# GateLoop attention and a multiplicative feed-forward block on one core: channels ordered (d h), gate tiles by parity of the unit, table functions in a fixed order

## The chip, the cores and the metric

The kernel runs on one NeuronCore of a Trainium2 chip. The metric is the device time of one execution in microseconds (us). PE is the matrix engine, DVE the vector engine, ACT the engine for table functions, POOL GpSimd, SP the engine whose queue issues most transfers.

## What is computed

Batch 4, 8 heads, 768 steps, 48 channels per head; then 3072 tokens of width 384 go through a feed-forward block of width 1024. The weights arrive in double precision, all else in float32.

```python
mag = np.sqrt(a_re * a_re + a_im * a_im)
scale = np.minimum(mag, 0.999) / (mag + 1e-06)
a_re_n, a_im_n = (a_re * scale, a_im * scale)
for t in range(S):
    new_re = ar * S_re - ai * S_im
    new_im = ar * S_im + ai * S_re
    S_re, S_im = (new_re + kv, new_im)
    y[:, :, t] = np.einsum('bhd,bhde->bhe', q[:, :, t], S_re)
...
a = x @ w1
b = x @ w2
h = a * b @ w3
return (h @ w_out).astype(np.float32)
```

## The kernel before

The work is cut into 8 units: a batch, half of its 768 steps (384), all heads. For each unit there are three kinds of work.

**Gates** (`gates`, L442 to L557). The 384 channels of all heads lie as 3 x 128 rows, 384 steps in the free direction. A chain of table functions (ACT), products and scans (DVE, POOL) turns the gates into decay and angle of every step and rotates q and k with them. The results are four tiles: k by cosine (`gR`), k by sine (`k`), q by cosine (`gA`), q by sine (`q`). `gZ` is scratch. All of `gA`, `gR`, `gZ`, `q`, `k` have one buffer, `re` and `im` two. The last lines of `gates` move the four tiles into a layout by head, `KL` and `QL`, with 2 x 48 rows and the head in the free direction. Channels are ordered (h d), so a head's 48 rows cross the borders of 128-row blocks and 40 transfers per unit are issued on SP (L551). Behind them on SP stand the loads of k and q of the next unit, and of the gates of the one after.

**Attention** (`scores`, `outputs`). For each of 3 chunks of 128 steps: transposes of `gR` and `k` (tp, L569) that ACT copies out (KT, L570), score products (sc, L574) that DVE masks (L575), outputs (y, L592 to L603) that ACT copies to xT (L605), and the state (kv on PE, T on DVE) for the next chunk.

**Feed-forward** (`ffn_ab`, `ffn_out`). Eight times a pair of products with w1 and w2 (m, L627), of which ACT copies one out (`a`) and DVE multiplies (`ab`, L632); then three output blocks (o, L637), copied by ACT and stored from ACT's own queue (L642).

Ahead of the units, the weights are converted from double to float32 in 36 pieces of at most 128 x 512 values (`convert`, L650 to L667: two operations on ACT, two on DVE, one on POOL, one on DVE), w3 and w_out are multiplied into one matrix (f, L719), and the gates of unit 0 run between them.

The program is written as: attention of unit u woven with the feed-forward of unit u-1 and the gates of unit u+1. The order on each engine is then chosen by the scheduler of the tile framework from its own estimates; engines and queues execute strictly in that order. The table functions on ACT belong to sets; a function of another set than the loaded one has an ACT_TABLE_LOAD in front of it.

```python
        nc.scalar.preload_act_table_set("natural_log_exp_and_others")
        for s in parts:
            act(out=A[:, s], in_=re[:, s], func=AF.Ln)
            act(out=r[:, s], in_=A[:, s], func=AF.Exp, scale=-1.0)
...
        nc.scalar.preload_act_table_set("trig_and_small")
        for s in parts:
            act(out=im[:, s], in_=im[:, s], func=AF.Arctan)
```

Of the kernel before, what the change touches and what calls it, by code (L numbers as in the profile page):

```python
# [15 lines left out]
PSUM = bass.MemoryType.PSUM  # L16

# [297 lines left out]
def kernel(  # L315
# [44 lines left out]
    KD = DM // P  # L360
    KF = FF // P
# [4 lines left out]
    LN_MAX = math.log(0.999)  # L366
# [20 lines left out]


# [23 lines left out]
    def rows(src, b):  # L412
        return src[b].rearrange("h d s -> (h d) s").rearrange("(f p) s -> p f s", p=P)

    def load_gates(u):
        b, h = divmod(u, 2)
        g = g_t[u] = {}
        for n, src in (("re", art), ("im", ait)):
            g[n] = two.tile([P, KD, TT], FP, tag=n, name=n)
            nc.sync.dma_start(out=g[n], in_=rows(src, b)[:, :, h * TT:(h + 1) * TT])  # L420

    def load_qkv(u):
        b, h = divmod(u, 2)
        g = g_t[u]
        g["q"] = one.tile([P, KD, TT], FP, tag="q", name="q")
        g["k"] = one.tile([P, KD, TT + UC], FP, tag="k", name="k")
        nc.sync.dma_start(out=g["k"][:, :, 0:TT], in_=rows(kt, b)[:, :, h * TT:(h + 1) * TT])
        nc.sync.dma_start(out=g["q"], in_=rows(qt, b)[:, :, h * TT:(h + 1) * TT])
# [12 lines left out]

    def gates(u, split):  # L442
# [3 lines left out]
        A, R = one.tile([P, KD, TT], FP, tag="gA", name="gA"), one.tile([P, KD, TT + UC], FP, tag="gR", name="gR")  # L446
# [5 lines left out]
        act = nc.scalar.activation  # L452
# [5 lines left out]
        nc.scalar.preload_act_table_set("natural_log_exp_and_others")  # L458
# [52 lines left out]
        nc.scalar.preload_act_table_set("trig_and_small")  # L511
# [28 lines left out]
        KL = two.tile([2 * D, H, TT + UC], FP, tag="KL", name="KL")  # L540
        QL = two.tile([2 * D, H, TT], FP, tag="QL", name="QL")
        L_t[u] = QL, KL, R, K2
        for dst, src in ((KL, (R, K2)), (QL, (A, q))):
            for hd in range(H):
                for x in range(2):
                    r0 = hd * D
                    while r0 < (hd + 1) * D:
                        f, p0 = divmod(r0, P)
                        n = min((hd + 1) * D - r0, P - p0)
                        d0 = x * D + r0 - hd * D  # L550
                        nc.sync.dma_start(out=dst[d0:d0 + n, hd], in_=src[x][p0:p0 + n, f])  # L551
                        r0 += n
        if u + 1 < NU:
            load_qkv(u + 1)
# [4 lines left out]
    def scores(u, c):  # L559
# [5 lines left out]
        for x, src in enumerate((R, K2)):  # L565
            if not last:
# [3 lines left out]
                nc.scalar.copy(out=KT[:, :, x], in_=tp.rearrange("p f c -> p (f c)").rearrange("p (h d) -> p h d", d=D))  # L570
# [63 lines left out]
    def ffn_out(u, t):  # L634
# [7 lines left out]
        nc.scalar.dma_start(out=out[r0:r0 + P, :], in_=o)  # L642
# [4 lines left out]
    LOAD = 512  # L647
    MIN_SQ = (1.125 * 2.0 ** -15) ** 2

    def convert(dst, pieces):  # L650

        r, m = dst.shape[1:]
        raw = two.tile([P, r, m, 2], I32, tag="raw", name="raw")
# [172 lines left out]
```

## Time and profile before

| | us |
|---|---|
| three runs | 766.9, 767.99, 768.14 (median 767.99) |
| the profiled execution's own time | 768.78 |
| its span in the trace | 767.0 |
| PE busy / DVE / ACT / POOL | 597.2 / 384.7 / 348.0 / 152.2 |

The profile tells for each engine when it was busy, what ended the idle time before an instruction, and which chain of work ended last. A busy PE is modelled time: matmuls overlap. A float32 matmul leaves two records on PE, a transpose one. "SPq" is the issue of transfers on SP.

### The profile page before, as it was taken

What the parts mean: (1) busy time and instruction counts of PE and PEld (TensorE: products, weight loads), DVE (VectorE), ACT (ScalarE), POOL (GpSimd) and SP (SyncE); (2) the same over time, 40 slices, a digit from 0 to 9 for tenths busy, and PEclk for the clock granted to TensorE, in tenths of its full rate; (3) what the DMA queues carried; (4) which work ended last, traced back from release to release, by engine and by line L of the source; (5) the groups of instructions that cost most, each with busy time, mean ns of one, the idle gap of its engine ahead of it and who ended that gap; (6) DMA issues with size and microseconds to landing.
All of it is one profiled execution on the core that took longest, in us unless ns stands there. A gap on an engine that the chain in (4) does not pass through costs nothing.

```text
span 767.0 us, 9438 instructions
## 1 busy us (share of the span) xinstructions
PE 597.2 (78%) x3514; PEld 376.7 (49%) x3514; DVE 384.7 (50%) x555; ACT 348.0 (45%) x466; POOL 152.2 (20%) x149
## 2 busy tenths in 40 slices
PE   0027795439599779879995899499888998899997
PEld 0013473215256446645663576257545655476554
DVE  4898737673424672485248336724671378131110
ACT  9977866543315542745263447334533463100110
POOL 5564313712202200230033011301120111000000
PEclk9999997658799999998999899789999999999999
DMA  8434545102335123312322240234013201300001
GB/s 298 143 110 156 182 123 171 56 27 90 111 95 187 52 58 88 116 49 75 110 81 77 70 148 11 73 101 126 11 34 93 82 11 33 94 20 11 23 0 35
DMA packets 49079, 65.81 MB, mean 86 GB/s; under 512 B 7552, under 2 KB 46464, under 8 KB 49024
## 3 DMA queue, kind: packets, MB, share of 16 engines
q1 hardware_dynamic: 45568, 60.40, 26.1%
q10 hardware_dynamic: 3456, 4.72, 1.7%
q8 instruction: 30, 0.49, 0.3%
q14 instruction: 25, 0.20, 0.1%
HBM read 41.42 MB, written 4.72 MB: 60 GB/s over the span
## 4 chain that ended last, share of the span: by engine, by line
PE 23%; DVE 21%; ACT 17%; SPq 15%; issue 13%; POOL 6%; DMA 4%; ACTq 0%; DVEq 0%; POOLq 0%
SPq L551 14%; PE m L627 12%; PE o L637 5%; DVE gZ L517 4%; DVE gZ L501 3%; DVE gR L487 3%; POOL cf L666 3%; POOL im L464 2%; PE sc L574 2%; PE kv L610 2%; ACT gZ L473 1%; DVE cf L665 1%; ACT L478 1%; ACT gZ L478 1%; DVE w3s L667 1%
## 5 line engine op out<-in xcount | busy, mean ns | idle before, releaser
L627 PE MATMUL m<-xT,w1s 128*128 128x384 f32 x384 | 153.2, 528 | 31.9 <-DVE w1s L667 14.6
L627 PE MATMUL m<-xT,w2s 128*128 128x384 f32 x384 | 148.0, 517 | 9.8 <-DVE w2s L667 4.9
L637 PE MATMUL o<-w3o,ab 128*128 128x384 f32 x384 | 130.1, 489 | 0.0
L627 PEld LDWEIGHTS m<-xT,w1s 128*128 128x128 f32 x384 | 74.0, 205 | 80.8 <-DVE w1s L667 17.4
L632 DVE TENSOR_TENSOR ab<-m,a 128x384 f32<-128x384 f32 x64 | 35.3, 554 | 140.8 <-PE m L627 140.6
L719 PE MATMUL f<-wo_s,w3s 128*128 128x384 f32 x128 | 50.0, 541 | 70.1 <-DVE w3s L667 70.1
L627 PEld LDWEIGHTS m<-xT,w2s 128*128 128x128 f32 x384 | 74.1, 200 | 59.5 <-issue 7.0
L631 ACT COPY a<-m 128x384 f32<-128x384 f32 x64 | 30.3, 477 | 149.2 <-PE m L627 134.7
L637 PEld LDWEIGHTS o<-w3o,ab 128*128 128x128 f32 x384 | 70.8, 190 | 45.1 <-issue 1.6
L719 PEld LDWEIGHTS f<-wo_s,w3s 128*128 128x128 f32 x128 | 25.4, 208 | 92.6 <-DVE w3s L667 75.3
L666 POOL TENSOR_TENSOR cf<-cf,low 128x512 int32<-128x512 int32 (+1 forms) x36 | 48.7, 1351 | 91.9 <-DVE cf L665 55.7
L574 PEld LDWEIGHTS sc<-QL,KL 96*128 96x128 f32 x384 | 51.8, 192 | 23.7 <-issue 12.2
L574 PE MATMUL sc<-QL,KL 96*128 96x128 f32 x384 | 56.7, 281 | 5.3 <-DMA QL<-q 4.5
L575 DVE COPY_PREDICATED A<-causal,sc 128x512 f32<-128x512 int32 x48 | 34.0, 732 | 47.2 <-PE sc L574 46.9
L439 POOL COPY V<-vr 128x128 f32<-128x128 f32 x24 | 10.6, 442 | 202.2 <-PE y L592 121.2
L528 ACT ACTIVATE re<-gZ 128x1152 f32<-128x1152 f32 (+1 forms) x10 | 9.6, 969 | 71.3 <-DVE gZ L525 71.3
L569 PE MATMUL tp<-ident,gR 128*128 128x128 f32 x60 | 12.2, 311 | 33.0 <-DVE gR L533 32.5
L464 POOL TENSOR_TENSOR im<-im,gR 128x1152 f32<-128x1152 f32 (+1 forms) x10 | 20.5, 2059 | 77.5 <-ACT gR L461 77.1
L610 PEld LDWEIGHTS kv<-V,KT 128*96 128x96 f32 x320 | 32.4, 174 | 5.1 <-issue 4.3
L610 PE MATMUL kv<-V,KT 128*96 128x64 f32 x320 | 34.1, 257 | 0.2 <-DVE T L614 0.2
L504 POOL TENSOR_TENSOR q<-q,gA 128x1152 f32<-128x1152 f32 (+1 forms) x10 | 21.8, 2182 | 60.4 <-DVE gA L498 60.4
L640 ACT COPY ot<-o 128x384 f32<-128x384 f32 x24 | 11.3, 474 | 48.8 <-PE o L637 48.1
(101 smaller groups left out, 837.8 us busy)
## 6 DMA issues: line engine op xcount, KB each, us to landing
raw<-in_w_dram SPq DMA_DIRECT2D x16, 512.0 KB, 3.8
re<-in_a_re_dram SPq DMA_DIRECT2D x8, 576.0 KB, 6.6
im<-in_a_im_dram SPq DMA_DIRECT2D x8, 576.0 KB, 3.8
k<-in_k_dram SPq DMA_DIRECT2D x8, 576.0 KB, 4.1
q<-in_q_dram SPq DMA_DIRECT2D x8, 576.0 KB, 5.6
vr<-in_v_dram SPq DMA_DIRECT2D x8, 576.0 KB, 4.2
out_dram<-ot ACTq DMA_DIRECT2D x24, 192.0 KB, 1.9
raw<-in_w_dram SPq DMA_DIRECT2D x32, 128.0 KB, 2.7
```

The lines of the kernel that those rows point to most:

```text
L464: nc.gpsimd.tensor_tensor(out=im[:, s], in0=im[:, s], in1=r[:, s], op=OP.mult)
L517: nc.vector.tensor_tensor_scan(out=Z[:, f], data0=im[:, f], data1=im[:, f], initial=0.0 if h == 0 else st_ang[:, u - 1, f, UC - 1:UC], op0 ...
L551: nc.sync.dma_start(out=dst[d0:d0 + n, hd], in_=src[x][p0:p0 + n, f])
L574: nc.tensor.matmul(out=sc[:, j], lhsT=KL[:, hd, w], rhs=QL[:, hd, w], start=True, stop=True)
L575: nc.vector.copy_predicated(out=A[:, x * H // 2:(x + 1) * H // 2], data=sc, mask=causal.rearrange("p (h t) -> p h t", h=1).to_broadcast([P ...
L610: nc.tensor.matmul(out=kv[:, hd], lhsT=KT[:, hd], rhs=V[:, hd], start=True, stop=True)
L627: nc.tensor.matmul(out=m, lhsT=w[:, f, j * P:(j + 1) * P], rhs=xT_t[u][:, f], start=(f == 0), stop=(f == KD - 1))
L631: nc.scalar.copy(out=a, in_=got[0])
L632: nc.vector.tensor_tensor(out=ab_t[u][:, j], in0=got[1], in1=a, op=OP.mult)
L637: nc.tensor.matmul(out=m, lhsT=ab_t[u][:, f, t * P:(t + 1) * P], rhs=w3o[:, f], start=(f == 0), stop=(f == KF - 1))
L666: nc.gpsimd.tensor_tensor(out=b, in0=b, in1=low, op=OP.add)
L719: nc.tensor.matmul(out=m, lhsT=w3_t[j][:, f], rhs=wo_s[:, f], start=(f == 0), stop=(f == KF - 1))
```

## The change

- The 384 channels of q, k and the gates are loaded in the order (d h): block f holds channels 16f to 16f+15 of all 8 heads (`load_rows`; three transfers per tile). A move to the head layout is then one transfer of 128 rows into 16 rows x 8 heads: 12 per unit.
- `gA`, `gR`, `q`, `k`, `KL`, `QL` of even units come from one pool, those of odd units from another (`sides`). The odd pool is opened when the conversions are over and lies where their scratch lay. `gZ` keeps one buffer. k and q of unit u+2 are requested when the gates of unit u+1 begin.
- The table functions of `gates` are chained: the scheduler must keep them in written order.
- The decay is accumulated as a product: exp ahead of the scan, minimum with 0.999, then a scan that multiplies; the correction step behind the scan (an Exp, a Ln, two DVE operations per unit) goes.
- Weights are converted in 18 pieces, mostly 128 x 1024, three raw buffers, one transfer each; the gates of unit 0 take a step at every piece.
- Outputs are stored from SP's queue.

```diff
+    def load_rows(dst, src, u):
+        b, h = divmod(u, 2)
+        for f in range(KD):
+            nc.sync.dma_start(out=dst[:, f, 0:TT], in_=src[b, :, DG * f:DG * (f + 1), h * TT:(h + 1) * TT].rearrange(
+                "h d s -> d h s"))
...
-        g["q"] = one.tile([P, KD, TT], FP, tag="q", name="q")
-        g["k"] = one.tile([P, KD, TT + UC], FP, tag="k", name="k")
+        g["q"] = sides[u % 2].tile([P, KD, TT], FP, tag="q", name="q")
+        g["k"] = sides[u % 2].tile([P, KD, TT + UC], FP, tag="k", name="k")
...
+    def chain(ins):
+
+        if chained:
+            tc.add_manual_dep(ins.ins, chained[-1].ins.name, ORDER, reason="tables")
+        chained[:] = [ins]
...
-        A, R = one.tile([P, KD, TT], FP, tag="gA", name="gA"), one.tile([P, KD, TT + UC], FP, tag="gR", name="gR")
+        A = sides[u % 2].tile([P, KD, TT], FP, tag="gA", name="gA")
+        R = sides[u % 2].tile([P, KD, TT + UC], FP, tag="gR", name="gR")
...
+        if 0 < u < NU - 1:
+            load_qkv(u + 1)
+        chain(nc.scalar.preload_act_table_set("natural_log_exp_and_others"))
...
-            ts(out=A[:, s], in0=A[:, s], scalar1=LN_MAX, scalar2=None, op0=OP.min)
-        for s in parts:
+            act(out=A[:, s], in_=A[:, s], func=AF.Exp)
+        yield
+
+        for s in parts:
+            ts(out=Z[:, s], in0=Z[:, s], scalar1=-1.0, scalar2=1.0, op0=OP.mult, op1=OP.add)
+            ts(out=A[:, s], in0=A[:, s], scalar1=0.999, scalar2=None, op0=OP.min)
...
-                    nc.vector.tensor_tensor_scan(out=r[:, f, w], data0=A[:, f, w], data1=Z[:, f, w], initial=0.0,
-                                                 op0=OP.add, op1=OP.subtract)
...
-        for s in parts:
-            act(out=A[:, s], in_=r[:, s], func=AF.Exp)
-            act(out=Z[:, s], in_=A[:, s], func=AF.Ln)
-        yield
-        for s in parts:
-            tt(out=Z[:, s], in0=r[:, s], in1=Z[:, s], op=OP.subtract)
+                    nc.vector.tensor_tensor_scan(out=A[:, f, w], data0=A[:, f, w], data1=Z[:, f, w], initial=1.0,
+                                                 op0=OP.mult, op1=OP.mult)
+        yield
+
+        for s in parts:
+            act(out=r[:, s], in_=A[:, s], func=AF.Ln)
             act(out=r[:, s], in_=r[:, s], func=AF.Exp, scale=-1.0)
-            stt(out=A[:, s], in0=Z[:, s], scalar=1.0, in1=A[:, s], op0=OP.add, op1=OP.mult)
...
+        KL = sides[u % 2].tile([2 * D, H, TT + UC], FP, tag="KL", name="KL")
+        QL = sides[u % 2].tile([2 * D, H, TT], FP, tag="QL", name="QL")
         L_t[u] = QL, KL, R, K2
         for dst, src in ((KL, (R, K2)), (QL, (A, q))):
-            for hd in range(H):
...
-                        nc.sync.dma_start(out=dst[d0:d0 + n, hd], in_=src[x][p0:p0 + n, f])
-                        r0 += n
...
+            for x in range(2):
+                for f in range(KD):
+                    r0 = x * D + f * DG
+                    nc.sync.dma_start(out=dst[r0:r0 + DG], in_=src[x][:, f])
...
-        nc.scalar.dma_start(out=out[r0:r0 + P, :], in_=o)
+        nc.sync.dma_start(out=out[r0:r0 + P, :], in_=o)
...
+        raw = cv3.tile([P, r, m, 2], I32, tag="raw", name="raw")
+        nc.sync.dma_start(out=raw.rearrange("p r m w -> p r (m w)"), in_=src)
...
+            hs = words(w).rearrange("(h e) m -> h e m", e=D)
+            for f, src in enumerate((hs[0:4, 0:LO], hs[4:8, 0:LO], hs[:, LO:D])):
+                got.append(lambda d=d, f=f, src=src: load_weight(d[:, f:f + 1], src))
...
+    conv.close()
+    sides[1] = fast.enter_context(tc.tile_pool(name="late", bufs=1))
+    load_qkv(1)
```

The scheduler moves much more than the diff shows. On ACT, the gates of unit 2 or a later one, before (a line number tells the function: L460 Ln, L461 Exp, L473 Ln, L513 Arctan, L478 Exp, L492 Exp, L493 Ln, L497 Exp):

```order
L460 ACT_TABLE_LOAD
L460 ACTIVATE gA<-re 128x1152
L461 ACT_TABLE_LOAD
L461 ACTIVATE gR<-gA 128x3x384
L605 COPY xT<-y 128x3x128
L473 ACT_TABLE_LOAD
L473 ACTIVATE gZ<-gZ,consts 128x1152
L513 ACT_TABLE_LOAD
L513 ACTIVATE im<-im 128x1152
L478 ACT_TABLE_LOAD
L478 ACTIVATE gZ<-gA,consts 128x1152
```

and now (all table functions of `gates` are called in L469; L478 and L527 are the two loads):

```order
L478 ACT_TABLE_LOAD
L640 COPY a<-m 128x384 x2
L579 COPY KT<-tp 128x8x48
L640 COPY a<-m 128x384 x2
L469 ACTIVATE gA<-re 128x1152
L469 ACTIVATE gR<-gA 128x3x384
L469 ACTIVATE gZ,st_low<-re,consts 128x1152
L649 COPY ot<-o 128x384
L614 COPY xT<-y 128x3x128
L649 COPY ot<-o 128x384
```

Ln and Exp now share one load, and Arctan and Sin the other: 16 loads instead of 84.

PE where the scores of unit 1 begin, before, from the last w2 product of unit 0 on:

```order
L627 MATMUL m<-xT,w2s 128x384 x3
L637 MATMUL o<-w3o,ab 128x384 x3
L574 MATMUL sc<-QL,KL 128x128
L637 MATMUL o<-w3o,ab 128x384 x2
L574 MATMUL sc<-QL,KL 128x128
L637 MATMUL o<-w3o,ab 128x384 x3
```

and now, from the last output blocks of unit 0 on (the tp rows are those of unit 2; unit 1's stand ahead of these rows):

```order
L646 MATMUL o<-w3o,ab 128x384 x11
L578 MATMUL tp<-ident,gR 128x128 x3
L578 MATMUL tp<-ident,k 128x128 x3
L578 MATMUL tp<-ident,gR 128x128 x3
L578 MATMUL tp<-ident,k 128x128 x3
L578 MATMUL tp<-ident,gR 128x128 x3
L583 MATMUL sc<-QL,KL 128x128 x16
```

The transposes of unit u+1 now stand ahead of the scores of unit u, so those scores wait for the gates of unit u+1; the feed-forward of unit u follows its own attention. The same stands ahead of the scores of units 3 to 6, with four or five tp rows.

SP behind the head moves of unit 0, now (raw are the weights' pieces):

```order
L563 DMA QL<-gA 16x8x384 x3
L563 DMA QL<-q 16x8x384 x3
L419 DMA re<-in_a_re_dram 128x1x384 x3
L662 DMA raw<-in_w_dram 128x8x256
L662 DMA raw<-in_w_dram 128x1x2048 x6
L419 DMA k<-in_k_dram 128x1x384 x3
```

The six pieces of w1 and w2 now stand as six transfers behind the moves of unit 0; before they were 64 transfers of 16 or 32 rows in the same place, and k and q of the next unit stood ahead of them.

## Rows read from the trace of the kernel before

**Rows 1.** The page, part 4: the chain that ended last, shares of the span by engine.

```profile
PE 23%; DVE 21%; ACT 17%; SPq 15%; issue 13%; POOL 6%; DMA 4%; ACTq 0%; DVEq 0%; POOLq 0%
```

**Rows 2.** Windows: stretch, busy us (instructions) of PE, PEld, DVE, ACT, POOL, TensorE clock, DMA share, GB/s.

```profile
0.00:30.00 30.00, 0.00 (x0) 0.00 (x0) 19.56 (x41) 27.61 (x46) 18.56 (x36) 1.00 0.73 256
...
150.00:200.00 50.00, 28.65 (x94) 16.39 (x94) 28.45 (x40) 19.03 (x30) 11.77 (x9) 0.70 0.21 63
...
309.00:381.00 72.00, 62.68 (x397) 39.71 (x396) 39.01 (x49) 32.70 (x41) 11.37 (x12) 0.95 0.27 82
```

**Rows 3.** The chain of waits: start us, length us, what.

```profile
199.58 1.27 POOL cf L666
...
232.16 1.33 SPq L551
...
378.74 2.13 DMA QL<-gA
382.31 1.17 ACT gA L460
...
453.81 1.17 ACT gA L460
```

**Rows 4.** Timeline of SP, the head moves of one unit: start us, us, engine, line, operation.

```profile
353.70 3.04 SPq L551 DMA_DIRECT2D KL<-gR  x5
...
379.37 0.59 SPq L551 DMA_DIRECT2D QL<-q  x1
```

**Rows 5.** Timeline of ACT in the gates that follow.

```profile
395.28 1.25 ACT L478 ACTIVATE gZ<-gA,consts 128x1152 f32<-128x1152 f32 x1
```

**Rows 6.** Timeline of DVE in the same gates.

```profile
391.52 1.36 DVE L477 SCALAR_TENSOR_TENSOR gA<-gZ,gA 128x1152 f32<-128x1152 f32 x1
...
397.36 3.00 DVE L487 TENSOR_TENSOR_SCAN gR<-gA,gZ 128x128 f32<-128x128 f32 x9
...
407.29 3.44 DVE L501 TENSOR_TENSOR gZ<-gA,gR 128x1152 f32<-128x1152 f32 x1 [0.47 <-ACT gR L497]
...
427.96 1.35 DVE L538 TENSOR_TENSOR q<-q,gZ 128x1152 f32<-128x1152 f32 x1
```

**Rows 7.** The chain of waits in the last unit: PE at work without a pause.

```profile
684.84 1.79 PE sc L574 x16
...
696.26 1.50 PE kv L610 x16
...
715.52 31.16 PE m L627 x96
746.67 15.49 PE o L637 x48
```

**Rows 8.** Timeline of PE, attention and transposes in the same period.

```profile
398.57 0.43 PE L592 MATMUL y<-A,V 128*32 128x128 f32 x8
...
400.46 5.43 PE L637 MATMUL o<-w3o,ab 128*128 128x384 f32 x16
407.67 2.20 PE L627 MATMUL m<-xT,w1s 128*128 128x384 f32 x6 [1.78 <-ACT xT L605]
...
446.23 0.49 PE L569 MATMUL tp<-ident,gR 128*128 128x128 f32 x3
...
447.43 0.49 PE L569 MATMUL tp<-ident,k 128*128 128x128 f32 x3
```

**Rows 9.** Timeline of DVE while weights are converted.

```profile
85.55 0.55 DVE L538 TENSOR_TENSOR q<-q,gZ 128x384 f32<-128x384 f32 x1
...
94.54 0.69 DVE L667 SCALAR_TENSOR_TENSOR w3s<-mag,cf 128x512 f32<-128x512 f32 x1 [1.44 <-POOL cf L666]
...
97.74 0.69 DVE L667 SCALAR_TENSOR_TENSOR w3s<-mag,cf 128x512 f32<-128x512 f32 x1 [1.45 <-POOL cf L666]
```

**Rows 10.** Groups of instructions by line and form: busy us, mean ns, idle before.

```profile
L513 ACT ACT_TABLE_LOAD x10 | 12.8, 1283 | 0.2
...
L575 DVE COPY_PREDICATED A<-causal,sc 128x512 f32<-128x512 int32 x48 | 34.0, 732 | 47.2 <-PE sc L574 46.9
```

More of the change, by code (lines that the diff above doesn't have):

```diff
@@ L386 @@
     ps_m = fast.enter_context(tc.tile_pool(name="ps_m", bufs=3, space=PSUM))
+    sides = [one, None]
     Ab = [singles.tile([P, H, C], FP, name=f"A{i}") for i in range(2)]
@@ L419, in load_gates @@
             g[n] = two.tile([P, KD, TT], FP, tag=n, name=n)
-            nc.sync.dma_start(out=g[n], in_=rows(src, b)[:, :, h * TT:(h + 1) * TT])
+            load_rows(g[n], src, u)
     def load_qkv(u):
@@ L510, in gates @@
         yield
-        nc.scalar.preload_act_table_set("trig_and_small")
+        chain(nc.scalar.preload_act_table_set("trig_and_small"))
         for s in parts:
@@ L569, in scores @@
                     nc.tensor.transpose(out=tp[:, f], in_=src[:, f, w], identity=ident)
-                nc.scalar.copy(out=KT[:, :, x], in_=tp.rearrange("p f c -> p (f c)").rearrange("p (h d) -> p h d", d=D))
+                nc.scalar.copy(out=KT[:, :, x], in_=tp.rearrange("p f c -> p (f c)").rearrange("p (d h) -> p h d", h=H))
             sc = ps_s.tile([P, H // 2, C], FP, tag="sc", name="sc")
@@ L641, in ffn_out, with convert @@
         r0 = u * TT + t * P
-        nc.scalar.dma_start(out=out[r0:r0 + P, :], in_=o)
-    LOAD = 512
+        nc.sync.dma_start(out=out[r0:r0 + P, :], in_=o)
+    LOAD = 1024
     MIN_SQ = (1.125 * 2.0 ** -15) ** 2
-    def convert(dst, pieces):
+    def convert(dst, src):
         r, m = dst.shape[1:]
-        raw = two.tile([P, r, m, 2], I32, tag="raw", name="raw")
-        for ps, src in pieces:
-            nc.sync.dma_start(out=raw[ps].rearrange("p r m w -> p r (m w)"), in_=src)
+        raw = cv3.tile([P, r, m, 2], I32, tag="raw", name="raw")
+        nc.sync.dma_start(out=raw.rearrange("p r m w -> p r (m w)"), in_=src)
         lo, hi = raw[:, :, :, 0], raw[:, :, :, 1]
-        low = two.tile([P, r, m], I32, tag="low", name="low")
-        mag = one.tile([P, r, m], FP, tag="mag", name="mag")
-        f = two.tile([P, r, m], FP, tag="cf", name="cf")
+        low = cv1.tile([P, r, m], I32, tag="low", name="low")
+        mag = cv1.tile([P, r, m], FP, tag="mag", name="mag")
+        f = cv2.tile([P, r, m], FP, tag="cf", name="cf")
         b = f.bitcast(I32)
@@ L700, in wo_work, with load @@
     def wo_work():
-        src = wo if wo.dtype == FP else wo.bitcast(I32)
-        src = src.rearrange("(i p) m -> p i m", p=P)
-        return [lambda i=i: load_weight(wo_s[:, i:i + 1], [(slice(0, P), src[:, i:i + 1])]) for i in range(KF)]
+        src = words(wo).rearrange("(i p) m -> p i m", p=P)
+        return [lambda i=i: load_weight(wo_s[:, i:i + 2], src[:, i:i + 2]) for i in range(0, KF, 2)]
     def w3_work(j):
-        src = w3t if w3t.dtype == FP else w3t.bitcast(I32)
         n = 1 if w3t.dtype == FP else 2
-        src = src.rearrange("(i p) m -> p i m", p=P)[:, :, n * j * P:n * (j + 1) * P]
-        def half(i):
-            if i == 0:
-                w3_t[j] = two.tile([P, KF, P], FP, tag="xT", name="w3s")
-            load_weight(w3_t[j][:, i:i + KF // 2], [(slice(0, P), src[:, i:i + KF // 2])])
-        return [lambda i=i: half(i) for i in (0, KF // 2)]
+        src = words(w3t).rearrange("(i p) m -> p i m", p=P)[:, :, n * j * P:n * (j + 1) * P]
+        def load():
+            w3_t[j] = two.tile([P, KF, P], FP, tag="xT", name="w3s")
+            load_weight(w3_t[j], src)
+        return [load]
     def fuse(j):
@@ L758 @@
         f()
-        if i % 2 == 0:
-            next(start, None)
+        next(start, None)
     for _ in start:
         pass
+    conv.close()
+    sides[1] = fast.enter_context(tc.tile_pool(name="late", bufs=1))
+    load_qkv(1)
     def interleave(a, b):
```

57 lines of the change are left out of this document (20 added, 37 removed).

## The prediction

> **What bounds the kernel now.** I read the chain that ended last, then the windows, then the timelines of the engines in one period. The chain by engine [rows 1] has no owner: PE 23%, DVE 21%, ACT 17%, the issue of transfers on SP 15%. A chain that changes hands like this is a loop over several engines. The windows [rows 2] show two regimes. From 150 to 200 us PE is busy 28.65 of 50 us at a clock of 0.70: the weights of the feed-forward are still being converted, the last piece on POOL at 199.58 [rows 3]. From 309 to 381 us PE is busy 62.68 of 72 us at 0.95, so it is nearly full but not the bound.
>
> The bound of the second regime is the gates. The Ln of one unit starts at 382.31, that of the next at 453.81 [rows 3]: a period of 71.5 us. Ahead of each stands the landing of the last QL move (378.74 + 2.13): `gA` has one buffer, so the next unit's gates start when this unit's `q` and `k` have left for the head layout. The loop is gate chain, then moves, then gate chain. The moves take from 353.70 to 379.97 on SP, 26.3 us for 40 issues of some 0.6 us [rows 4]. The chain goes from 382.31 to the end of the last rotation, 427.96 + 1.35 = 429.3 [rows 3, 6]: 47.0 us.
>
> PE's own pace, where nothing holds it: 31.2 us for 96 records of m, 15.5 us for 48 of o, 1.8 for 16 of sc, 1.5 for the 16 of one chunk's kv [rows 7], and 1.9 us from the start of one chunk's y to what follows it [rows 8]. A unit needs 31.2 + 15.5 + 3 x 1.8 + 3 x 1.9 + 2.5 x 1.5 (the last chunk of every second unit has no kv), and five transposes of three records at 0.49 [rows 8]: 64.0 us. That is the floor under the 71.5.
>
> **What the change does to the gate chain.** *Table loads.* 84 become 16, 1.28 us each [rows 10]. On the chain: the load before the first Exp, 1.3; ahead of the Exp of Z now stand Arctan and two loads, so it starts at 395.28 though its input was there at 391.52 + 1.36 = 392.88 [rows 5, 6], 2.4; the load before Sin, 1.3. *Scan.* Now the scan ends at 400.36 and the product that follows starts at 407.29 [rows 6]: Exp, Ln, two DVE operations and loads, 6.9 us. After the change an Ln and an Exp of some 1.17 us stand there, 2.3: 4.6 saved. An Exp ahead of the scan is new, 1.2. Together 47.0 - 1.3 - 2.4 - 1.3 - 4.6 + 1.2 = **38.6 us**. The multiplying scan has no row; I take the adding one's 3.0 us [rows 6], with double that, or half, as ends (plus or minus 3 us in a chain that later hides behind PE).
>
> *Moves.* 12 instead of 40: at 0.6 us each 7 us of issue, if an issue of 128 rows costs like one of 48; I take no gain from it, since with tiles by parity no gate waits for a move, and the moves have a whole unit until their scores. The stores on SP stand ahead of later moves; they too have that unit of slack, so I cost them at nothing. If the moves became three times as dear they would still end before the next unit's scores.
>
> **Until the scores of unit 1.** The program changes most here. In the old kernel they start at about 234 us, with all output blocks of unit 0 still to do [rows 3]. Now the odd tiles lie where the conversions had their scratch, so the gates of unit 1 start when the last piece is converted, and PE's order puts the transposes of unit 2 ahead of the scores of unit 1: two gate chains in a row, with PE idle.
>
> - The gates of unit 0 end at 86 us on DVE now [rows 9]; nearly the same conversions stand among them after the change. I keep 85.
> - Nine pieces remain, and unit 0's six masked copies and five state updates of some 0.7 us [rows 10], 8 us. Half a piece takes 3.2 us now, of which DVE waits 1.45 for POOL [rows 9]. Between 3.5 us (no wait) and 6.4 us for a whole one I take 4.2, near the low end, because the new order puts the next piece's first two DVE operations where the wait was: 38 us. The conversions end at 85 + 8 + 38 = 131.
> - The loads of w1 and w2 must keep up: in the first 30 us 256 GB/s arrived [rows 2], 4.1 us for a piece of 1 MB, as much as its conversion. I add 3 us: **134 us**. The end on the other side is a transfer that runs at a quarter of that pace, the first rival, with 744 us in place of 721. The Trainium skill speaks for that end, on the page "DMA: Bandwidth & Descriptors", sections "Why a DMA increments its semaphore by 16 and not by 1" and "Rules for kernel authors": a transfer is spread over the largest number of engines up to 16 that divides the slowest dimensions of both its sides. No run here shows it so far.
> - First chain 38.6 us, with eight `ab` products between: 41. The second can run its Ln, Exp and POOL product beside the end of the first (5 us less) but its two Relu wait for `gZ` (3 us more): 36.5; then the rest of unit 2's transposes, 1.2 us from one to the next [rows 8], 2.5. Scores of unit 1 at 134 + 41 + 36.5 + 2.5 = **214 us**.
>
> **From there to the end.** Units 1 to 5 run beside gates. These must not take longer than the rest of the unit: they start some 5 us after the scores and need 38.6 us plus the `ab` products, so they end within m, well ahead of the transposes that wait for them. PE becomes the bound, with three stalls. Four or five transposes stand in a row, each waiting for ACT to copy the one before: 1.2 instead of 0.49 us [rows 8], 3.2 us. The third xT copy stands behind an Exp pair on ACT, which waits for DVE: now 1.78 us [rows 8], I take 3. Between `ab` products DVE has a block of scans longer than an `ab` pair, and three PSUM buffers bridge about one pair of products, 31.2 / 8 = 3.9: 2.7 us. And the clock, 0.95 now with some 9 us of stalls in the period [rows 2]: 2.5 us. 64.0 + 11.4 = **75 us**, five times 375. The old kernel wove its transposes and scores into the feed-forward, so each of its periods was shorter. Unit 6 has no gates and no transposes beside it: 64. Unit 7, with the 4.8 us between the last o (746.67 + 15.49) and the end of the span [rows 7]: 66.
>
> Sum: 214 + 375 + 64 + 66 = 719 us of span. The profiled execution took 768.78 at a span of 767.0, so 721; the median of the runs, 767.99, is 0.1% under that execution, which I leave out.
>
> Where the 47 us go: scores of unit 1 are 20 us earlier, and PE has done 15.5 us of o by then; the last unit follows without gates; units 1 to 5 lose 3.5 us each against now.
>
> **Rivals.**
>
> 1. *The loads of w1 and w2 crawl.* Each piece is one transfer whose outer dimension on the DRAM side is 4 or 8 heads, and if the transfer is dealt to as many DMA engines, it has 4 or 8 of 16. At 256 GB/s for a share of 0.73 [rows 2] one engine does 22 GB/s: 12 us for each of four pieces, 6 for two, 60 us behind the moves of unit 0, which leave at 90. Conversions end at 157, the time is **744**. For it: the form of the six transfers. Against it: no row has such a transfer. Chance 0.33. (This is the rule of the Trainium skill named above.)
> 2. *PE's stalls in the units stay small*, because the copies and products arrive in time: 67 us per unit, 5 x 8 less, **681**. For it: in 309 to 381 PE's gaps come from the gate loop that goes. Chance 0.12.
> 3. *The order costs more*: DVE's scans and POOL's products slow each other (the product behind the scan takes 3.44 us, other products on DVE 1.36 [rows 6]), `ab` comes late, 81 us per unit: **751**. Chance 0.07.
> 4. *Slower than before.* Gates of unit 1 wait for all conversions. If these stay at their old pace, with the last at 200 us instead of 134 [rows 3], the time is 721 + 66 = **787**; it is slower from 181 us on. For it: two gate chains follow them with nothing else for PE. Against it: the old pieces were held up by DVE's queue, which had the gates of unit 1 in it. Chance 0.05.
>
> **Chances and range.** My forecast has 0.42, with 705 to 735 as its own range. Faster than before by over 0.2% (what a measurement can tell from no change) are it and the rivals 1 to 3: 0.94. Slower is rival 4, 0.05; the 0.01 left is a conversion that ends just at 181 us. The range from 680 to 756 takes in rivals 1 to 3 and the ends of the unknown prices; what is left out is rival 4 and the tails, under 0.2.
>
> **What the profile will show.** If right: 16 table loads; Ln to Ln in the late units no longer behind a QL landing; the last conversion near 134 us; scores of unit 1 near 214; a period near 75 us whose PE gaps end at KT, xT and `ab`. If rival 1: the pieces of w1 and w2 land some 12 us apart with DVE waiting for them. It is wrong if the first scores of unit 1 come after 240 us, if PE waits for gR in the late units, or if SP's moves are waited for by the scores.

## The result and the profile after

The changed kernel takes **748.55 us** (median of 4 runs, 743.49 to 749.98), the kernel before 768.07 beside it: a ratio of 0.9725, 95% interval 0.9666 to 0.9783. It is faster by 2.7%, where 721 us, or 6.1%, were forecast. The profiled execution took 749.98 us at a span of 748.2; the sums below are made against that span.

The page of the changed kernel, parts 1 and 4: busy time, and the chain by engine, to be held against [rows 1].

```profile
PE 587.1 (78%) x3514; PEld 381.9 (51%) x3514; DVE 354.0 (47%) x491; ACT 256.2 (34%) x362; POOL 147.9 (20%) x131
...
PE 49%; DVE 20%; ACT 10%; DMA 8%; issue 7%; POOL 2%; SPq 2%; DVEq 0%; ACTq 0%; POOLq 0%
```

The chain has an owner now: PE rose from 23% to 49%, the issue on SP fell from 15% to 2%. The share of DMA rose from 4% to 8%. The chain in order of time shows where it lies:

```profile
118.05 19.86 DMA raw<-in_w_dram
...
142.91 28.51 DMA raw<-in_w_dram
...
176.86 1.24 DVE w2s L674
178.12 1.17 ACT gA L469
...
257.43 4.59 PE sc L583 x27
```

Two stretches of the chain, 48 us together, are transfers of raw pieces of w1 and w2. The last piece is done at 178.1; the Ln of unit 1 starts in the same microsecond; the scores of unit 1 follow 79 us later. The windows of the changed kernel (columns as in [rows 2]):

```profile
90.00:110.00 20.00, 16.07 (x82) 10.80 (x82) 3.70 (x4) 7.80 (x13) 2.46 (x2) 1.00 0.74 149
...
140.00:165.00 25.00, 3.64 (x64) 2.90 (x64) 5.50 (x7) 4.10 (x5) 7.46 (x7) 0.50 0.57 131
...
210.00:257.00 47.00, 22.29 (x96) 14.35 (x97) 29.92 (x36) 25.27 (x31) 7.80 (x3) 0.71 0.79 112
...
329.00:404.00 75.00, 67.33 (x413) 43.46 (x412) 34.01 (x48) 23.91 (x35) 8.22 (x11) 0.97 0.33 63
```

From 140 to 165 us no engine does much: the kernel waits for weights. From 210 to 257 PE is half idle behind the second gate chain. From 329 us on it is nearly full, 67.33 of 75 us against 62.68 of 72 [rows 2].

The first scores of each unit, read from the timelines of PE, make the balance:

| us | before | after | difference |
|---|---|---|---|
| scores of unit 1 | 224.5 | 257.2 | +32.7 |
| units 1 to 5, five periods | 363.9 | 366.0 | +2.1 |
| unit 6 | 75.5 | 59.4 | -16.1 |
| unit 7 to the end of the span | 103.1 | 65.6 | -37.5 |
| span | 767.0 | 748.2 | -18.8 |

The first scores come 33 us later, the pace is the same, and 54 us are saved in the last two units. Part of the first and the last row is order and cancels: in the old kernel a unit's scores stood ahead of the output blocks of the unit before (15.5 us), so more work was left behind them.

### The profile page after: what moved, and what is told of

It is laid out like the page before. It is cut to its first block, busy times and chain, and to the rows that moved or that the text cites. A ratio compares the mean times of both kernels' runs of the same rounds, so it can differ in the third digit from the quotient of the medians.

```text
span 748.2 us, 8868 instructions
## 1 busy us (share of the span) xinstructions
PE 587.1 (78%) x3514; PEld 381.9 (51%) x3514; DVE 354.0 (47%) x491; ACT 256.2 (34%) x362; POOL 147.9 (20%) x131
## 3 DMA queue, kind: packets, MB, share of 16 engines
q1 hardware_dynamic: 44512, 65.10, 43.5%
## 4 chain that ended last, share of the span: by engine, by line
PE 49%; DVE 20%; ACT 10%; DMA 8%; issue 7%; POOL 2%; SPq 2%; DVEq 0%; ACTq 0%; POOLq 0%
PE m L636 18%; PE o L646 16%; DMA raw<-in_w_dram 6%; PE sc L583 5%; DVE gZ L533 3%; PE kv L619 3%; DVE gA L508 3%; PE tp L578 2%; ACT gZ L469 2%; ACT gR L469 2%; POOL cf L673 2%; SPq L419 1%; PE f L713 1%; DVE cf L670 1%; ACT KT L579 1%
## 5 line engine op out<-in xcount | busy, mean ns | idle before, releaser
L636 PE MATMUL m<-xT,w1s 128*128 128x384 f32 x384 | 141.7, 506 | 20.6 <-ACT xT L614 12.7
L636 PE MATMUL m<-xT,w2s 128*128 128x384 f32 x384 | 136.0, 490 | 5.3 <-ACT a L640 2.9
L646 PEld LDWEIGHTS o<-w3o,ab 128*128 128x128 f32 x384 | 72.5, 192 | 49.1 <-issue 2.1
L713 PEld LDWEIGHTS f<-wo_s,w3s 128*128 128x128 f32 x128 | 27.4, 218 | 81.4 <-DVE w3s L674 59.0
L673 POOL TENSOR_TENSOR cf<-cf,low 128x1024 int32<-128x1024 int32 (+1 forms) x18 | 47.3, 2630 | 59.4 <-DVE cf L672 30.4
L579 ACT COPY KT<-tp 128x384 f32<-128x384 f32 x40 | 19.1, 478 | 99.5 <-PE tp L578 98.7
L668 ACT ACTIVATE low<-raw 128x1024 int32<-128x1024 uint32 (+1 forms) x18 | 19.8, 1102 | 80.5 <-POOL cf L673 42.5
L601 PE MATMUL y<-A,V 128*32 128x128 f32 x384 | 20.5, 285 | 26.4 <-ACT xT L614 26.4
L670 DVE TENSOR_SCALAR cf<-raw 128x1024 int32<-128x1024 int32 (+1 forms) x18 | 16.9, 942 | 40.2 <-DMA raw<-in_w_dram 33.8
L614 ACT COPY xT<-y 128x384 f32<-128x384 f32 x24 | 11.3, 473 | 62.9 <-PE y L612 41.4
```

The lines of the kernel that those rows point to most:

```text
L636: nc.tensor.matmul(out=m, lhsT=w[:, f, j * P:(j + 1) * P], rhs=xT_t[u][:, f], start=(f == 0), stop=(f == KD - 1))
L646: nc.tensor.matmul(out=m, lhsT=ab_t[u][:, f, t * P:(t + 1) * P], rhs=w3o[:, f], start=(f == 0), stop=(f == KF - 1))
L673: nc.gpsimd.tensor_tensor(out=b, in0=b, in1=low, op=OP.add)
L713: nc.tensor.matmul(out=m, lhsT=w3_t[j][:, f], rhs=wo_s[:, f], start=(f == 0), stop=(f == KF - 1))
```

## The experiments

Times are medians of all runs of a kernel; "conversions end" is the end of the last operation on w2s in the profiled execution; the period is the mean of units 1 to 5.

| kernel | conversions end | scores of unit 1 | period | time |
|---|---|---|---|---|
| after | 178.1 | 257.2 | 73.2 | 748.55 |
| e1, loads by head | 172.5 | 250.1 | 72.1 | 736.66 |
| e6, DVE in turn | 173.3 | 252.7 | 72.3 | 739.9 |
| e5, both | 144.3 | 225.0 | 73.3 | 719.1 |
| e2, loads of 2 heads | 216.0 | 293.6 | 72.6 | 784.27 |
| e4, tables unordered | 190.5 | 278.8 | 76.0 | 785.73 |
| e8, single gate tiles | 198.5 | 244.2 | 82.3 | 796.55 |
| e10, e5 and scores first | 144.8 | 220.0 | 68.9 | 693.88 |
| e11, scores first alone | 182.4 | 238.8 | 72.2 | 724.44 |
| e13, e10 and moves of 32 rows | 143.8 | 217.7 | 68.3 | 690.81 |

**E1: the loads by head.**

```diff
-            for f, src in enumerate((hs[0:4, 0:LO], hs[4:8, 0:LO], hs[:, LO:D])):
+            for f, src in enumerate(([hs[j, 0:LO] for j in range(4)], [hs[4 + j, 0:LO] for j in range(4)],
+                                     [hs[j, LO:D] for j in range(H)])):
```

> Theory (each of the six loads of w1 and w2 runs on as many DMA engines as its outer dimension counts heads, 4 or 8): one load per head, of 32 or 16 rows, spreads over all 16; a piece lands some 6 us after its issue, the last conversion ends near 140 us in place of 178, the scores of unit 1 start near 218 in place of 257, periods stay near 73 us, the time is 705 to 715 us. Rival (the conversions are late because a raw buffer comes free late, or because the moves of unit 0 fill the DMA engines; the form of the load is indifferent): the last conversion stays at 170 to 178, the time at 740 to 750.

736.66 us, ratio 0.9589 (0.9544 to 0.9635): faster than the changed kernel, but the conversions end only 5.6 us earlier. Neither theory foresaw that. The waits of DVE from 90 to 131 us in this kernel (us in total, times, longest) name a second holder:

```profile
DVE T L623 <- PE kv L619: 12.9, 1, 12.9
DVE A L584 <- PE sc L583: 5.4, 3, 4.1
```

Attention of unit 0 stands in DVE's queue ahead of the last pieces and waits for PE. The changed kernel has the same from 90 to 118 us:

```profile
DVE T L623 <- PE kv L619: 11.3, 1, 11.3
...
DVE A L584 <- PE sc L583: 2.5, 3, 2.0
DVE T L625 <- PE kv L619: 2.5, 1, 2.5
```

**E2: the opposite dose.**

```diff
+            for f, src in enumerate(([hs[0:2, 0:LO], hs[2:4, 0:LO]], [hs[4:6, 0:LO], hs[6:8, 0:LO]],
+                                     [hs[0:4, LO:D], hs[4:8, LO:D]])):
```

> Opposite dose: each load of w1 and w2 is cut in two, over 2 heads where it was 4, over 4 where it was 8; bytes and row lengths are the same. Theory (engines = heads in the outer dimension, always the same first ones): a 1 MB piece has 2 or 4 engines instead of 4 or 8; four pieces take some 10 us more each, two some 5 us more, the last conversion ends near 225 us and the time is 785 to 800 us. Rival (size of a transfer, or what stands ahead of it, sets its landing): two smaller transfers land no later than one, the time is 735 to 750.

784.27 us (ratio 1.0187, 1.0136 to 1.0238), conversions to 216.0: the theory, a little milder. DVE's first operation on the last five pieces in the changed kernel, then on the last four in E2 (timeline, with idle time ahead and what ended it):

```profile
133.19 0.69 DVE L670 TENSOR_SCALAR cf<-raw 128x1024 int32<-128x1024 int32 x1 [9.26 <-DMA raw<-in_w_dram]
...
138.00 1.18 DVE L670 TENSOR_SCALAR cf<-raw 128x1024 int32<-128x1024 int32 x1 [1.85 <-DMA raw<-in_w_dram]
...
150.94 0.69 DVE L670 TENSOR_SCALAR cf<-raw 128x1024 int32<-128x1024 int32 x1 [9.22 <-DMA raw<-in_w_dram]
...
164.77 0.69 DVE L670 TENSOR_SCALAR cf<-raw 128x1024 int32<-128x1024 int32 x1 [10.28 <-DMA raw<-in_w_dram]
...
171.52 0.69 DVE L670 TENSOR_SCALAR cf<-raw 128x1024 int32<-128x1024 int32 x1 [3.18 <-DMA raw<-in_w_dram]
```

```profile
156.96 0.69 DVE L675 TENSOR_SCALAR cf<-raw 128x1024 int32<-128x1024 int32 x1 [3.56 <-DMA raw<-in_w_dram]
176.99 0.69 DVE L675 TENSOR_SCALAR cf<-raw 128x1024 int32<-128x1024 int32 x1 [14.34 <-DMA raw<-in_w_dram]
199.49 0.69 DVE L675 TENSOR_SCALAR cf<-raw 128x1024 int32<-128x1024 int32 x1 [16.80 <-DMA raw<-in_w_dram]
210.32 0.70 DVE L675 TENSOR_SCALAR cf<-raw 128x1024 int32<-128x1024 int32 x1 [5.13 <-DMA raw<-in_w_dram]
```

The pieces of 4 heads at 150.94 and 164.77 come 13 to 14 us behind the one before in the changed kernel, their like in E2 20 to 22.5 us. The last piece, of 8 heads, comes 6.8 us behind, and 10.8.

**E3 and E7: the forms by themselves.** Kernels of transfers alone: w1 as 4 heads, as 2 x 2 heads, as 4 x 32 rows, as 8 heads, as 8 x 16 rows, and w3's form. In E3 transfers of other tiles ran beside them, so that a form's price can't be read from it (4 heads took 22 us in that company, 4 x 32 rows 8); E7 puts each behind the landing of the one before.

> Only transfers, one form after the other, each waiting for the one before it; nothing of the reference is computed, the output is filled with zeros. Theory: 1 MB over 4 heads lands after about 11 us, as two loads of 2 heads after about 20, as four of 32 rows after 5 or less; over 8 heads after about 6, as eight of 16 rows after 5 or less; the form of w3 after 5 or less. For the 12 moves of 128 rows against the 40 of 16 to 48 rows, 1.19 MB either way: if the moves of the whole kernel cost more DMA time because of their form, the 12 take 10 us or more and the 40 are bounded by issue, some 24 us of 0.6 us each, at a lower busy share; if the form is indifferent both busy the engines equally long.

> The forms of transfer again, now each strictly behind the landing of the one before; nothing of the reference is computed, the output is filled with zeros. Theory: from issue to landing 1 MB over 4 heads takes 18 to 24 us, over 2 x 2 heads 25 to 40, as four loads of 32 rows 5 to 8, over 8 heads 9 to 13, as eight loads of 16 rows 6 to 9 (bounded by the issues), in the form of w3 5 to 9. The six KL moves of a unit as 6 transfers of 128 rows take 6 us or more though few issues, as 20 transfers of 16 to 48 rows 12 to 15 us, bounded by issue at 0.6 us each. The three loads of a gate tile by head and row: no slower than the one transfer of 128 x 3 rows, if the form is indifferent there.

The windows of E7, one per form in the order named (columns: DVE and POOL busy, clock, DMA share of 16 engines, GB/s):

```profile
116.40:132.60 16.20, 0.14 (x1) 0.00 (x0) 1.00 0.20 65
132.60:159.50 26.90, 0.11 (x2) 0.00 (x0) 1.00 0.11 39
159.50:166.90 7.40, 0.20 (x2) 0.00 (x0) 1.00 0.63 142
166.90:178.70 11.80, 0.17 (x2) 0.00 (x0) 1.00 0.39 89
178.70:189.00 10.30, 0.15 (x1) 0.00 (x0) 1.00 0.73 102
189.00:194.60 5.60, 0.15 (x1) 0.00 (x0) 1.00 0.61 187
```

The same 1 MB takes 16.2, 26.9, 7.4, 11.8, 10.3 and 5.6 us. The shares of 16 engines come to 3.2, 1.8, 10, 6.2, 11.7 and 9.8 busy engines on average, issue and landing included: for 4, 2 and 8 heads the average stays below 4, 2 and 8. For most of each of these three stretches (10, 23 and 7 us by the start and length of each packet in the trace) exactly 4, 2 and 8 packets are in flight. Two transfers of 2 heads in flight together still show 1.8, so they share the same two. This agrees with the rule of the Trainium skill that the prediction named (page "DMA: Bandwidth & Descriptors", section "Why a DMA increments its semaphore by 16 and not by 1"), which adds that such a transfer, issued from SP, takes the lowest-numbered engines. Which engines they are no run here shows. The theory's range for 4 heads, 18 to 24, was too high: 16.2; that for eight loads of 16 rows, 6 to 9, too low: 10.3. Three loads of a gate tile by head and row took 4.4 us, the one of before 4.0: by itself that part of the change costs next to nothing.

**E5 and E6: DVE in turn, with and without the loads by head.** The two halves of a conversion are written apart, so that a piece's first two DVE operations come ahead of the last one of the piece before, and a chain keeps that order; unit 0's masked copies and state updates come behind the last piece.

```diff
+        in_turn(nc.vector.tensor_scalar(out=b, in0=hi, scalar1=3, scalar2=0x3FFFFFFF, op0=OP.logical_shift_left,
+                                        op1=OP.bitwise_and))
...
+            behind(nc.vector.copy_predicated(
+                out=A[:, x * H // 2:(x + 1) * H // 2], data=sc,
```

> The loads by head of the first experiment, and DVE's operations on the pieces in a fixed order: the first two of a piece, then the last of the piece before; the masked copies and state updates of unit 0 behind the last piece. Theory (with loads by head what holds the conversions is DVE's own queue: attention of unit 0 stands ahead of the pieces and waits for PE, and a piece no longer overlaps the next): pieces 4 to 4.5 us apart from 92 us on, the last one ends at 130 to 140 us, the scores of unit 1 start at 210 to 220, 700 to 715 us. Rival (ACT and POOL with their single buffers, or the raw buffers, set the pace at 6 us and more): the last one at 155 or later, 722 to 740 us.

> The same fixed order on DVE, with the loads as the change has them, over 4 and 8 heads. Theory (both causes are needed; the loads of 4 and 8 engines take some 60 us behind the moves of unit 0): the last conversion ends at 155 to 180 us, 728 to 750 us. Rival (the order on DVE alone holds the conversions, the loads could keep up): the last one at 130 to 140, 700 to 715 us.

E6: 739.9 us (0.9615, 0.9573 to 0.9658), conversions to 173.3. E5: **719.1 us** (0.9343, 0.9298 to 0.9388), conversions to 144.3. Undoing one holder gives 5 us of earlier conversions, undoing both 34: each hid behind the other. What of the order's part comes from the pieces and what from attention standing behind them was not separated. E5's time is above the theory's 700 to 715 by as much as its conversions are behind 130 to 140. DVE's last operations on pieces of w1 and w2 in E5:

```profile
118.20 1.23 DVE L695 SCALAR_TENSOR_TENSOR w1s<-mag,cf 128x1024 f32<-128x1024 f32 x1 [2.25 <-POOL cf L690]
...
143.03 1.23 DVE L695 SCALAR_TENSOR_TENSOR w2s<-mag,cf 128x1024 f32<-128x1024 f32 x1 [2.24 <-POOL cf L690]
```

Five steps in 24.8 us, 5.0 a piece. The start is late too: the first piece behind unit 0's moves waits 11.8 us for its load, and the window from 91 to 104 us (columns as in [rows 2]) has all 16 DMA engines full (a share of 1.09: some packets overlap).

```profile
91.00:104.00 13.00, 11.81 (x47) 7.24 (x45) 1.36 (x2) 3.36 (x6) 3.21 (x1) 0.97 1.09 236
```

```profile
104.12 0.69 DVE L686 TENSOR_SCALAR cf<-raw 128x1024 int32<-128x1024 int32 x1 [11.76 <-DMA raw<-in_w_dram]
```

**E4: the tables unordered.** Everything else as after the change.

```diff
-        if chained:
-            tc.add_manual_dep(ins.ins, chained[-1].ins.name, ORDER, reason="tables")
```

> The fixed order of the table functions is taken out, all else is as after the change: 88 table loads instead of 16, some 92 us more on ACT. Theory (in the late periods PE is the bound and gates hide behind it, before them two chains stand on the path): the two gate chains ahead of the scores of unit 1 grow by some 10 us each, the late periods by 0 to 4 us where ACT copies come late; 765 to 785 us. Rival (table loads lie in ACT's idle time everywhere): 748 to 755. Other rival (the order itself is what takes the gates off the bound): periods back above 80, over 800.

785.73 us (ratio 1.0191, 1.015 to 1.0232): slower than before the change, and just above the theory's 765 to 785. Groups of ACT_TABLE_LOAD, first of the changed kernel, then of E4:

```profile
L478 ACT ACT_TABLE_LOAD x8 | 10.3, 1283 | 0.9 <-PEq L813 0.7
L527 ACT ACT_TABLE_LOAD x8 | 10.3, 1283 | 0.1
```

```profile
L467 ACT ACT_TABLE_LOAD x71 | 91.1, 1283 | 1.2
```

With 8 at each of two other lines that makes 87 in E4, 16 in the changed kernel. Conversions end 12 us later, the two gate chains take 88 us instead of 79, and the five periods 76.0 instead of 73.2, 14 us: together 35 us, as much as the spans differ (783.6 and 748.2). The theory had put 20 us into the two chains, which took 9, and had not seen that the conversions would end later. Without the fixed order the change loses all of its gain.

**E8: single gate tiles.** `q`, `k`, `gA`, `gR` come from one tile again; KL and QL stay by parity.

```diff
-        A = sides[u % 2].tile([P, KD, TT], FP, tag="gA", name="gA")
+        A = one.tile([P, KD, TT], FP, tag="gA", name="gA")
```

> q, k, gA and gR have one tile again for all units (their loads behind the moves of the unit before, as in the kernel before); KL and QL stay by parity, all else is as after the change. Theory (tiles by parity cost the start more than they give later, since the odd ones wait for the end of all conversions and the gate chain of 39 us plus moves and reload of 20 to 25 would fit a period of 73): the gates of unit 1 run among the conversions, the scores of unit 1 start before 225 us, periods stay at 72 to 77, 710 to 730 us. Rival (without the second tiles the loop of gates, moves and reload binds again): periods of 78 or more, 745 to 790 us.

796.55 us (ratio 1.0346, 1.0296 to 1.0396): the rival. The scores of unit 1 are 13 us earlier than after the change, but periods are 74 and 87 us in turns. The waits of SP, and of PE, in two of them:

```profile
SPq L419 <- PE tp L578: 18.0, 1, 18.0
```

```profile
PE sc L583 <- DVE A L584: 19.4, 3, 13.5
```

The reload of `k` waits not only for the moves but for the transposes, which read the same tile and stand late in PE's queue; the gates start late, their DVE work falls on the masked copies, and PE waits for those. Tiles by parity are worth 9 us a period, and without them too the change is a loss: it needs both parts.

**E10 and E11: scores first.** The transposes of a unit may not stand ahead of the last scores of the unit before; E10 on top of E5, E11 on the changed kernel.

```diff
+                    if u - 1 in last_sc:
+                        tc.add_manual_dep(t.ins, last_sc[u - 1].ins.name, ORDER, reason="scores first")
```

> On top of the loads by head and the fixed order on DVE: on PE the transposes of a unit may not stand ahead of the last scores of the unit before. Theory (the two gate chains of 80 us in a row ahead of the scores of unit 1 are one chain too many, and only PE's order makes it so): the scores of unit 1 start at 195 to 205 us in place of 225, the feed-forward of unit 1 some 15 us earlier; the transposes, now between matmuls, no longer wait for ACT's copies, 0 to 3 us less in a period; 690 to 708 us. Rival (DVE's copies and state updates of unit 1 now stand before the end of the gates of unit 2, and the transposes of unit 2 then hold the feed-forward of unit 1 as long): the scores are early, the time stays at 712 to 722.

> The same order on PE on the kernel after the change, with its loads over 4 and 8 heads and its free order on DVE. Theory (what the order gives does not hang on when the conversions end): the scores of unit 1 start at 225 to 238 us in place of 257, the time falls by as much as on the other kernel, to 720 to 735 us. Rival (gates of unit 2 and attention of unit 1 collide on DVE): 740 to 750.

E10: **693.88 us** (0.9024, 0.8995 to 0.9053). E11: 724.44 us (0.9408, 0.9368 to 0.9448). Both gain 24 to 25 us, as the theory's times had it, but not by its mechanism. In E10 the scores of unit 1 come at 220.0, only 5 us earlier than in E5, because there the feed-forward of unit 0 already filled PE beside the second chain (37.3 of 41 us busy from 184 to 225). The gain lies in the periods, 68.9 instead of 73.3. E11, whose profiled execution took 732.09 us, has the scores of unit 1 at 238.8, 18 us earlier than the changed kernel, just outside the theory's 225 to 238; but its first period is 85.5 us instead of 72.0, and the next four average 68.9 us instead of 73.5. The waits of PE over the late units, E5 first, then E10:

```profile
PE tp L591 <- ACT KT L592: 8.0, 14, 0.6
PE m L649 <- DVE ab L654: 7.1, 7, 1.5
...
PE m L649 <- ACT xT L627: 2.7, 2, 1.4
```

```profile
PE m L653 <- DVE ab L658: 2.2, 4, 0.7
PE m L653 <- ACT a L657: 1.2, 3, 0.4
PE tp L593 <- ACT KT L596: 0.9, 2, 0.6
```

Transposes that stand in a row wait for ACT's copies, 8.0 us; woven into the feed-forward they wait 0.9, and the products wait less for `ab` too, 2.2 us instead of 7.1.

**E12 and E13: the moves.** E12 runs only the moves of a KL tile; E13 is E10 with the moves of units 1 to 7 cut into four of 32 rows.

> Only the six moves that make a KL tile, 1.19 MB with rows of 387 numbers, in other forms, each form behind the landing of the one before; nothing of the reference is computed, the output is filled with zeros. In one earlier run the form of the change (128 rows to 16 partitions of 8 rows) had the DMA engines busy for 80% of 12.6 us, the form before (16 to 48 rows to as many partitions) for 30% of 14.9. Theory A (several rows that go to one partition, one behind the other, are slow): 64 rows to 8 partitions and 32 rows to 4 are as busy in sum or busier; 16 rows of one head to 16 partitions, and 128 rows to the same 128 partitions, are as cheap as the form before, 60 to 80 engine-us against 160. Theory B (16 partitions close together are slow whatever stands behind them): the form by head, 16 rows to 16 partitions, is as dear as that of the change. Theory C (size and overlap of the transfers): 128 rows to the same 128 partitions is as dear as the change's form.

Windows of E12 (columns as for E7): 6 transfers of 128 rows to 16 partitions; 12 of 64 to 8; 24 of 32 to 4; 48 of 16 rows of one head to 16; the form before; 128 rows to the same 128 partitions.

```profile
109.40:122.00 12.60, 0.08 (x1) 0.00 (x0) 1.00 0.89 123
122.00:144.00 22.00, 0.22 (x2) 0.00 (x0) 1.00 0.46 54
144.00:163.60 19.60, 0.10 (x1) 0.00 (x0) 1.00 0.22 61
163.60:191.00 27.40, 0.20 (x2) 0.00 (x0) 1.00 0.13 38
195.50:209.50 14.00, 0.15 (x1) 0.00 (x0) 1.00 0.32 85
209.70:216.00 6.30, 0.15 (x1) 0.00 (x0) 1.00 0.52 189
```

Share times 16 times length: 179, 162, 69, 57, 72 and 52 engine-us for the same bytes. None of the three theories holds: 32 rows to 4 partitions, also 8 rows to each, are cheap, so it is not the rows to one partition alone; the form by head is cheap, so it is not the 16 partitions alone; the plain copy is cheap, so it is not the size alone. What makes 64 and 128 rows dear stays open. A rival that no run varies by itself would fit all six: many engines at work at once on a few neighbouring partitions. For most of the time there are 16 packets or more in flight to 16 partitions at a time in the first form and 8 or more to 8 in the second, of 0.16 and 0.19 us each on average; 4 or 5 to 4 partitions in the third, of 0.08 us; the form by head mostly has fewer in flight, and the plain copy spreads its 16 over 128 partitions, with 0.04 and 0.06 us.

```diff
+                    for p in range(0, P, P if u == 0 else 32):
+                        r0, n = x * D + f * DG + p // H, (P if u == 0 else 32) // H
+                        nc.sync.dma_start(out=dst[r0:r0 + n], in_=src[x][p:p + n * H, f])
```

> On top of the fastest kernel so far (694 us; loads by head, fixed order on DVE, scores first): the moves of units 1 to 7 by 32 rows to 4 partitions, 48 instead of 12 a unit, the form that kept the DMA engines busy for 22% of 20 us by itself where the change's took 89% of 13. Theory (engines wait some 3 us at a time, named issue in the chain, while the DMA engines are full of moves; seven such gaps of 1.9 to 3.4 us stand in the chain from 365 to 575 us, 20 us together): most of the gaps shrink to about 1 us as in the kernel before, 8 to 14 us less, 680 to 687 us. Rival (the gaps do not come from the moves, and 32 us of issues on SP, with loads and stores behind them, still fit a unit): 691 to 697. Other rival (the moves now land so late that scores wait for them, or loads of q and k behind them are late): over 700.

**690.81 us** (0.8996, 0.8982 to 0.901), against 693.88 in E10: 3 us, between the theory and its rival, and with intervals that overlap. The chain of E10 from 365 us on has seven gaps named "issue" of 1.9 us and more, two of which are

```profile
367.80 3.41 issue
...
383.51 3.14 issue
```

In E13's chain one such gap is left there. But the theory took the gaps for one thing, and the timelines of the engines show at least two. At 383.51 no engine stops: DVE is in the middle of a scan, with the DMA engines idle (share 0.00). The same scan, first in E10, then in E13:

```profile
383.31 3.41 DVE L546 TENSOR_TENSOR_SCAN gZ<-im,st_ang 128x384 f32<-128x384 f32 x1
```

```profile
376.81 3.41 DVE L546 TENSOR_TENSOR_SCAN gZ<-im,st_ang 128x384 f32<-128x384 f32 x1
```

Three of E10's seven gaps, and all three of 3.3 us that E13's chain has from 215 us on, are such scans; E13 has them as often and as long, only its chain runs elsewhere meanwhile. A fourth gap, at 463.23, is DVE idle for 2.1 us ahead of `gR`, and E13 has that too, with 2.3. The other three are stops of PE in the middle of the products y (timeline of PE in E10):

```profile
371.21 0.44 PE L618 MATMUL y<-A,V 128*32 128x128 f32 x4 [3.41 <-issue]
```

They lie at 367.80, 505.06 and 574.39 us, 8 us together, with the DMA engines at 1.06, 0.37 and 0.04, so it is not full engines alone. The trace has a load of instructions inside each of the first two, and inside or just ahead of the third; that PE waits for its instructions would fit, but no wait shows it. E13, with the DMA queues at 35.8% of the span instead of 48.4%, has no stop of PE of that kind behind 200 us. But PE's waits are no shorter as a whole: from 288 to 620 us they come to 14 us in both kernels, in E13 6.3 of them for `ab` and 3.8 for xT, so the five periods gain only 3 us together. And the issue of its moves, 48 a unit, now stands in the chain with 9% of the span. E13 is the fastest kernel of this study, 10.0% below the kernel before.

## Why the prediction was wrong, point by point

The direction was right, and 748.55 lies in the range, but the size was not: 2.7% for 6.1%. The failing step is one number, the end of the conversions: the term that lets the loads of w1 and w2 keep up for 3 us, and beside it the 8 us for unit 0's attention. The first scores of unit 1 came at 257.2, past the 240 us that the forecast itself had named as a sign of being wrong.

- **The end of the conversions: forecast 134 us, measured 178.1.** "The loads of w1 and w2 must keep up ... I add 3 us" failed: pieces of 4 heads came 13 to 14 us apart, and DVE waited 33.8 us for the five pieces behind the first. The number that I used, 256 GB/s over the first 30 us [rows 2], belongs to other forms of transfer; E7 shows 65 GB/s for this one. The sum before it, 85 + 8 + 38, failed as well: the 8 us of unit 0's attention are busy time, but DVE's queue waits with them for PE, 16.3 us from 90 to 118. E1 and E6 take away one holder each and gain 5 us, E5 takes both and gains 34. In E5, where attention stands behind the pieces, the sum without its 8 us gives 126. The 18 us from there to 144.3 are about a piece of 5.0 us instead of 4.2, nine times, and the 11.8 us for a first load that lands late while the DMA engines are full.
- **The first rival is what happened**, with its sign as written: pieces some 12 us apart with DVE waiting. It gave 157 us and 744 us; it was given 0.33 against 0.42 although its rule stood beside it, and only the lack of a row spoke against it. Its 12 us a piece were 13 to 14, and it too lacked the second holder.
- **Two gate chains: forecast 80 us, measured 79.1** (257.2 - 178.1). In E1, E5 and E6 it is 77.6, 80.7 and 79.4. The load count of 16 was right, and so was the price of the multiplying scan: 2.96 us, as much as the adding one [rows 6].
- **The period: forecast 75 us, measured 73.2.** The stalls were of the kinds named and smaller: from 329 to 549 us, three periods, PE waited 6.3 us for KT (3.2 a period were forecast), 4.2 for `ab` (2.7 a period), 3.0 for xT (3 a period). One stop of 3.5 us in the products y, of the sort shown under E13, was of no kind named. The clock was 0.96 to 0.97.
- **Unit 6 and unit 7: 64 and 66 forecast, 59.4 and 65.6 measured.** In unit 6 PE is busy for 58.4 of 59 us at a clock of 1.00 (window 623 to 682): that is less work than the floor of 64.0 had counted. The five transposes lie ahead of it, and the last output products, four of 48 records, behind the next scores.
- **The sum again**: 44 us later conversions, 1 less in the chains, 9 less in five periods, 5 less in unit 6 and 7: 719 + 44 - 1 - 9 - 5 = 748, the span. With both holders gone E5 takes 719.1 us, where the forecast had 721: that is luck, its later start (225.0 for 214) and its faster units cancel.
- **Moves and stores at no gain and no cost**: no run isolates them. From 178 us on the chain of the changed kernel holds one landing of a move, 5.9 us at 409, and none of a store, and the issue price of 0.6 us held (1.9 us for three). That their load on the DMA engines would rise was not foreseen. The 11.8 us in E5, behind unit 0's moves, are probably its price; no run changes those moves.
- **Two readings of the kernel before were wrong.** Its scores of unit 1 start at 224.5, not 234, and with the first output products already done; its conversions end at 214.4 on DVE, not at 200, since the POOL operation at 199.58 is not the last. Timelines of PE and DVE:

```profile
224.46 0.39 PE L574 MATMUL sc<-QL,KL 96*128 96x128 f32 x2
```

```profile
213.72 0.69 DVE L667 SCALAR_TENSOR_TENSOR w2s<-mag,cf 128x512 f32<-128x512 f32 x1 [1.93 <-POOL cf L666]
```

  So the forecast's 214 us was only 10 us earlier than before, not 20, and the rival of conversions at their old pace would have come to 721 + 80 = 801 us. The sum of the forecast itself uses neither.
- The third rival's 81 us a unit did not come. Its mechanism may be there at a small size: a scan of the kind shown under E13 overlaps a product of POOL and takes 3.4 us, the two beside it don't and take 1.0.
- The forecast took PE's order, with unit 2's transposes ahead of unit 1's scores, as part of the change and costed it rightly; E10 and E11 show that it was worth 24 us to undo.

## What to carry over

Ahead of a transfer's size, look at the outermost dimension on both sides: 1 MB over 4 heads took 16 us where four transfers of 32 rows took 7.4. Busy time of an operation in an in-order queue is not its price: ask what it waits for and what stands behind it. When two holders end within a few microseconds of each other, undoing one shows little, here 5 of 34 us; test them together.

## What had not been expected of the hardware

- Moving rows inside SBUF, 1.19 MB: 128 rows into 16 partitions of 8 rows each kept the DMA engines busy for 179 engine-us, the form before for 72. Fewer transfers were dearer for the engines, though cheaper for SP (3.9 us of issue against 12.6). In the kernel the share of the span that the queues of data took went from 27.8% to 43.5% at the same 65.1 MB.
- A scan on DVE over 128 x 384 values takes 1.0 us, but 2.8 to 3.4 us where it overlaps POOL's product `k<-k,gR` for some 2 us or more: one of three in each of units 1 to 7 in E10. The kernel before has the same, 3.1 to 3.5 us in units 2 to 7. That the one holds up the other is likely; no run takes them apart.
- PE stops in the middle of a row of products for 1.9 to 3.4 us without a wait that the profile names, three times in E10 from 365 us on, in E13 not once behind 200. A load of instructions lies inside or just ahead of each stop. The cause is not shown.
